# Grouped-query decode attention: larger units, one uniform TensorE loop, and the last weights loaded last

## The chip, the cores and the metric

The kernel runs on one core of a Trainium2 chip. The metric is the device time of one execution in microseconds (us). The span in a profile is the time from the first to the last instruction; the times are 1.7 to 2.9 us longer. One core is in use, so there is no second die to compare with: a run is called slow when it is over 1.5% above the fastest run of its kernel. Ratios are the mean time of one kernel's fast runs over that of the kernel before in the same rounds, so they are not quite the ratios of the medians that I quote.

## The reference

Two attention blocks, A and B, each with batch 4 and one query token. 32 query heads share 8 key heads (4 per key head). The head size is 128, the cache has 8192 keys. A attends to all of them, B only to the last 2048. All data are bf16.

```python
q = (x @ wq).reshape(B, 1, 32, 128).transpose(0, 2, 1, 3)
scores = einsum("bhqd,bhkd->bhqk", q, repeat(k, 4)) * 128 ** -0.5   # B: the last 2048 keys only
o = einsum("bhqk,bhkd->bhqd", softmax(scores), repeat(v, 4))
y = o.transpose(0, 2, 1, 3).reshape(B, 1, 32 * 128) @ wo
# the result: concatenate([A, B], axis=-1)
```

A's K and V are 134 MB, B's 34 MB, the weights 17 MB. Every byte is used once, so the DMA time is a floor.

## The kernel before

Work is cut into 40 units with 2 MB of K and 2 MB of V each: 8 for B (four key heads of one batch), then 32 for A (one key head of one batch). K and V have four slots each. In A a partition holds 64 consecutive keys, one contiguous row of 16 KB.

```python
units = []
for gg in range(HKV // SB):            # B: four key heads
    for b in range(Bn):
        units.append(dict(P=1, b=b, S=2, J=NT // 2, CPT=2 * REP, ...))
for g in range(HKV):                   # A: one key head
    for b in range(Bn):
        units.append(dict(P=0, b=b, S=1, J=NT, CPT=REP, ...))
```

TensorE transposes K (two bf16 keys ride as one fp32), VectorE and ScalarE copy the result out of PSUM, TensorE multiplies it with the queries (S), and the weighted values (PV) follow one unit later. A unit's order on TensorE is this list:

```python
TOKENS = [("T", 0), ("T", 1), ("OT",), ("T", 2), ("T", 3), ("S", 0), ("S", 1), ("X",),
          ("T", 4), ("T", 5), ("S", 2), ("S", 3), ("PV", 0), ("PV", 1), ("OL",),
          ("T", 6), ("T", 7), ("S", 4), ("S", 5), ("PV", 2), ("PV", 3), ("S", 6), ("S", 7), ("OPJ",)]
```

A slot is loaded again when TensorE has read it. The last two K are loaded one after the other, ahead of the last three V:

```python
def sp_K(u):
    waits = [("T", tjob_idx[(u - NKS, NB - 1)])] if u >= NKS else []     # NKS = 4 slots
def sp_V(u):
    waits = [("PV", (u - NVS) * NQ + NQ - 1)] if u >= NVS else []        # NVS = 4 slots
```

TensorE loops over 28 of A's units, four units a turn, to keep its program short. B's query is made first; A's query is made in pieces within B's units.

## Time and profile before

| | before |
|---|---|
| time, median | 449.34 us (448.96 to 450.16, 4 runs) |
| span | 447.8 us |
| DMA data packets | from 1.8 to 440.2 us |
| tail after them | 7.6 us |
| mean granted clock | 0.797 |

From the page of the kernel before: busy time of the engines, the TensorE clock in tenths, DMA and GB/s in 40 slices of the span, and the chain that ended last by engine.

```profile
PE 373.4 (83%) x6783; PEld 339.4 (76%) x6783; DVE 195.9 (44%) x451; ACT 179.2 (40%) x202; POOL 40.1 (9%) x126
...
PEclk9996569989886899866596689867875986788596
DMA  8999999999999999999999999999999999999991
GB/s 337 411 415 438 413 421 415 420 421 423 423 422 421 425 422 425 424 429 427 427 427 430 430 424 426 430 428 427 429 426 427 426 430 429 426 424 430 430 403 65
...
DMA 54%; PE 35%; issue 4%; ACT 3%; DVE 2%; POOL 0%; ACTq 0%; POOLq 0%
```

The DMA row is full in every slice but the first and the last: the kernel is held by DMA. TensorE is close behind it.

The end, by stretches of 10 us: busy us (and instructions) of PE, PEld, DVE, ACT and POOL, then the granted clock, the DMA share and GB/s.

```profile
420.00:430.00 10.00, 9.94 (x136) 7.80 (x135) 4.20 (x9) 4.24 (x5) 0.94 (x3) 0.68 1.01 428
430.00:440.00 10.00, 8.94 (x207) 8.45 (x205) 5.80 (x12) 5.50 (x7) 1.15 (x3) 1.00 0.80 326
```

DMA is full until two microseconds before its end.

### The profile page before, as it was taken

To read this page: it belongs to the slowest core of one execution; us is meant where nothing else is said; L and a number is where in the kernel's file an instruction comes from. 1 tells how busy PE (TensorE), PEld (TensorE's weight loads), DVE (VectorE), ACT (ScalarE), POOL (GpSimd) and SP (SyncE) were. 2 spreads that over 40 slices of the span, in tenths; PEclk is the share of its full clock that TensorE was granted. 3 is DMA by queue.
4 is the path that set the end of the run, shared out by engine and by line. 5 is a ranking of instruction groups with operands and counts; after the bars stand their busy time and mean duration, and the time that the engine had idled before them with its cause. 6 is when DMAs were issued, how large, how long until landed. Compare 5 with 4: busy or idle time off the path is not lost.

```text
span 447.8 us, 14767 instructions
## 1 busy us (share of the span) xinstructions
PE 373.4 (83%) x6783; PEld 339.4 (76%) x6783; DVE 195.9 (44%) x451; ACT 179.2 (40%) x202; POOL 40.1 (9%) x126
## 2 busy tenths in 40 slices
PE   0685199899676999988998998899889998988997
PEld 0685199768561898878898887879878987878896
DVE  0354055656440455434363444344443544344363
ACT  1163045435330464434264434334442543435261
POOL 1100000001100011000010001000110100010010
PEclk9996569989886899866596689867875986788596
DMA  8999999999999999999999999999999999999991
GB/s 337 411 415 438 413 421 415 420 421 423 423 422 421 425 422 425 424 429 427 427 427 430 430 424 426 430 428 427 429 426 427 426 430 429 426 424 430 430 403 65
DMA packets 17270, 185.01 MB, mean 413 GB/s; under 512 B 1860, under 2 KB 2392, under 8 KB 4824
## 3 DMA queue, kind: packets, MB, share of 16 engines
q1 hardware_dynamic: 15096, 178.27, 94.4%
q10 hardware_dynamic: 2080, 6.30, 3.5%
q8 instruction: 22, 0.36, 0.3%
q14 instruction: 8, 0.07, 0.0%
q0 software_dynamic: 64, 0.01, 0.0%
HBM read 184.56 MB, written 0.01 MB: 412 GB/s over the span
## 4 chain that ended last, share of the span: by engine, by line
DMA 54%; PE 35%; issue 4%; ACT 3%; DVE 2%; POOL 0%; ACTq 0%; POOLq 0%
DMA K_sb<-in_A_k_cache_dram 41%; PE ps L332 19%; DMA W<-in_A_wq_dram 7%; DMA W<-in_B_wo_dram 6%; PE ps L397 6%; PE ps L371 5%; PE ps L483 3%; ACT KT_sb L341 3%; PE ps L278 1%; DVE KT_sb L340 1%; DVE Dt L543 0%; DVE M L505 0%; ACT PT L554 0%; PE ps L474 0%; PE ps L438 0%
## 5 line engine op out<-in xcount | busy, mean ns | idle before, releaser
L341 ACT ACTIVATE KT_sb<-ps 128x1024 bf16<-128x1024 bf16 x160 | 163.0, 1023 | 244.9 <-PE ps L332 243.1
L332 PE MATMUL ps<-identf,K_sb 128*128 128x128 f32 x1280 | 217.1, 329 | 32.9 <-DMA K_sb<-in_A_k_cache_dram 17.5
L332 PEld LDWEIGHTS ps<-identf,K_sb 128*128 128x128 f32 x1280 | 179.0, 170 | 46.2 <-DMA K_sb<-in_A_k_cache_dram 18.6
L340 DVE COPY KT_sb<-ps 128x512 int32<-128x512 int32 x160 | 110.4, 690 | 138.9 <-PE ps L332 137.7
L397 PE MATMUL ps<-PT,V_sb 128*128 128x4 bf16 (+1 forms) x2560 | 76.2, 165 | 3.6 <-DMA V_sb<-in_A_v_cache_dram 1.8
L371 PEld LDWEIGHTS ps<-RQc,KT_sb 128*128 128x128 bf16 x2048 | 72.9, 100 | 4.5 <-ACT KT_sb L341 1.2
L371 PE MATMUL ps<-RQc,KT_sb 128*128 128x8 bf16 x2048 | 74.3, 167 | 0.9 <-ACT KT_sb L341 0.8
L397 PEld LDWEIGHTS ps<-PT,V_sb 128*128 128x128 bf16 x2560 | 70.8, 97 | 3.9 <-DMA V_sb<-in_A_v_cache_dram 2.0
L575 POOL PARTITION_ALL_REDUCE LB<-L x40 | 17.3, 432 | 155.2 <-DVE L L566 155.2
L514 POOL PARTITION_ALL_REDUCE MB<-M x32 | 11.9, 371 | 173.3 <-DVE M L505 173.3
L483 PE MATMUL ps<-W,OL 128*4 128x512 bf16 x60 | 22.5, 537 | 4.8 <-DMA W<-in_B_wo_dram 4.8
L592 DVE TENSOR_TENSOR OTg<-ps,RL 128x4 bf16<-128x4 f32 (+1 forms) x40 | 6.9, 173 | 40.2 <-PE ps L397 40.2
L505 DVE TENSOR_REDUCE M<-ps 128x4 f32<-128x256 f32 (+1 forms) x40 | 19.1, 477 | 10.8 <-PE ps L371 10.8
L566 DVE TENSOR_REDUCE L<-PT 128x4 f32<-128x256 bf16 (+1 forms) x40 | 21.9, 547 | 3.3 <-ACT PT L554 2.8
L371 PE MATMUL ps<-RQB,KT_sb 128*128 128x16 bf16 x512 | 18.6, 171 | 2.1 <-issue 1.2
L371 PEld LDWEIGHTS ps<-RQB,KT_sb 128*128 128x128 bf16 x512 | 17.9, 99 | 3.0 <-issue 1.5
L554 ACT ACTIVATE PT<-Dt 128x256 bf16<-128x256 f32 (+1 forms) x40 | 18.1, 452 | 4.0 <-DVE Dt L543 2.0
L483 PEld LDWEIGHTS ps<-W,OL 128*4 128x4 bf16 x60 | 5.6, 104 | 15.3 <-issue 8.7
L278 PE MATMUL ps<-xT,W 128*128 128x4 bf16 x256 | 7.4, 165 | 10.9 <-DMA W<-in_A_wq_dram 10.6
L278 PEld LDWEIGHTS ps<-xT,W 128*128 128x128 bf16 x256 | 7.0, 101 | 11.1 <-DMA W<-in_A_wq_dram 10.7
L543 DVE TENSOR_TENSOR Dt<-ps,MB 128x256 f32<-128x256 f32 x32 | 13.3, 415 | 0.5 <-POOL MB L514 0.5
L257 PE MATMUL ps<-ident,xo_sb 4*128 4x4 bf16 x8 | 0.6, 170 | 14.2 <-POOL identf L617 14.2
(49 smaller groups left out, 64.6 us busy)
## 6 DMA issues: line engine op xcount, KB each, us to landing
K_sb<-in_A_k_cache_dram SPq DMA_DIRECT2D x32, 2048.0 KB, 32.0
V_sb<-in_A_v_cache_dram SPq DMA_DIRECT2D x31, 2048.0 KB, 36.0
K_sb<-in_B_k_cache_dram SPq DMA_DIRECT2D x16, 1024.0 KB, 28.2
V_sb<-in_B_v_cache_dram SPq DMA_DIRECT2D x16, 1024.0 KB, 28.2
W<-in_B_wq_dram SPq DMA_DIRECT2D x1, 4096.0 KB, 12.9
W<-in_A_wq_dram SPq DMA_DIRECT2D x1, 4096.0 KB, 30.0
W<-in_A_wo_dram ACTq DMA_DIRECT2D x8, 512.0 KB, 10.5
W<-in_B_wo_dram SPq DMA_DIRECT2D x1, 2048.0 KB, 29.1
```

Of the source, the lines that this page charges most:

```text
L278: ins = pe.matmul(out=bk[:, hl * Bn:(hl + 1) * Bn], lhsT=W1wq[:, c, hq * DH:(hq + 1) * DH], rhs=xT[:, P, c, :], start=(c == 0), stop=(c == ...
L332: ins = pe.transpose(out=bkf[:, pi * 128:(pi + 1) * 128], in_=K_sbf[:, slot, t0:t0 + 2, :].rearrange("p t d -> p (t d)"), identity=identf[ ...
L340: return e.tensor_copy(out=KT_sb.bitcast(I32)[:, tj % NKT, :], in_=bkf.bitcast(I32)[:, :])
L341: return e.activation(out=KT_sb[:, tj % NKT, :], in_=bk[:, :], func=ACTF.Copy)
L371: ins = pe.matmul(out=stb[:, t * CPT:(t + 2) * CPT], lhsT=ktv[:, pi, :, e], rhs=rhs, start=(e == 0), stop=(e == 1))
L397: ins = pe.matmul(out=otb[:, s * CPT:(s + 1) * CPT], lhsT=V_sb[:, vs, t, :], rhs=pt_cols(u, t * CPT, CPT), start=(j == 0), stop=(j == J - 1))
L483: ins = pe.matmul(out=opb[0:Bn, 0:D], lhsT=OL[:, i // REP, i % REP, :], rhs=wo_view[:, wg + i // REP, i % REP, :], start=(P == 1 and first ...
L505: return dve.tensor_reduce(out=M1[:, 0:NC].rearrange("p (s h) -> p s h", h=CPT), in_=stb[:, 0:NT * CPT].rearrange("p (s j h) -> p s h j", ...
L543: return dve.tensor_tensor(out=Dt[:, 0:NT * CPT].rearrange("p (s j h) -> p s j h", s=S, h=CPT), in0=stb[:, 0:NT * CPT].rearrange("p (s j h ...
L554: return act.activation(out=PT[:, u % NPT, 0:NW], in_=Dt[:, 0:NW], func=ACTF.Exp, scale=scale)
L566: return dve.tensor_reduce(out=L1[:, 0:NC].rearrange("p (s h) -> p s h", h=CPT), in_=PT[:, u % NPT, 0:NT * CPT].rearrange("p (s j h) -> p ...
L575: return pool.partition_all_reduce(LB[:, 0:NC], L1[:, 0:NC], channels=128, reduce_op=ReduceOp.add)
```

## The change

The intent: fewer and longer DMA rows in A (32 KB instead of 16), one form for all units, one TensorE loop over everything, and an end in which the last bytes to land (1 MB of output weights) need little work. There are 20 units with 4 MB of K and 4 MB of V: 4 for B (all eight key heads of a batch) and 16 for A (two key heads of a batch). K and V have two slots each. The core of the diff, with cuts:

```diff
-    NKS, NVS, NKT, NPT = 4, 4, 4, 4
+    units = [dict(P=1, b=b) for b in range(Bn)]
+    units += [dict(P=0, b=b, gp=gp) for gp in range(NSEG) for b in range(Bn)]
...
-        K_sb = sb("K_sb", [128, NKS, NT, DH], BF16)          # 4 slots of 2 MB
-        V_sb = sb("V_sb", [128, NVS, NT, DH], BF16)
+        K_sb = sb("K_sb", [128, 2, NT, DH], BF16)            # 2 slots of 4 MB
+        V_sb = sb("V_sb", [128, 2, NT, DH], BF16)
...
+        for P in (1, 0):                                     # both queries ahead of the loop
+            pe_job_xT(P)
+            for i in range(NQP):
+                pe_job_QP(P, i)
+            pe_job_perm(P)
+        op("pe", None, waits=[("E", perm_idx[0]), ("setup",)])
...
+        TOK = []
+        pc = 0
+        for k in range(NJ):                                  # NJ = 16
+            TOK.append(("T", k))
+            if k < 2:
+                TOK.append(("PV", k))
+                pc += 1
+            else:
+                TOK.append(("S", k - 2))
+                if pc < NC:                                  # NC = 8
+                    TOK.append(("PV", pc))
+                    pc += 1
+        TOK += [("S", NJ - 2), ("S", NJ - 1)]
...
+                else:                                        # values two units behind, of nothing at first
+                    pe_PV(u - 2, tok[1], waits=[("V", u - 2) if u >= 2 else None] if tok[1] == 0 else [])
...
+            w = [("T", tjob_idx[(u - 2, NJ - 1)])] if kind == "K" else [("PV", (u - 2) * NC + NC - 1)]
...
+        for P in (1, 0):                                     # 8 MB of query weights ahead of the first K
+            op("sp", dma(V_sb[:, 1 - P, :, :].rearrange("p t d -> p (t d)"), WQ[P]...), inc=("WQ", P))
+        kv_load("K", 0)
+        for u in range(1, NU + 1):
+            if u < NU:
+                kv_load("K", u)
+            kv_load("V", u - 1)
...
+        for i, n in enumerate(WCH):                          # the last 1 MB of output weights, behind the last V
+            op("sp", dma(Wl_sb[:, h0:h0 + n, :], src), inc=("WL", i))
...
-            with nc.Fori(0, len(turns), engines=[mybir.EngineType.PE]):      # 7 turns of 4 units
+            with nc.Fori(0, n_turn, engines=[mybir.EngineType.PE]):          # 10 turns of 2 units
```

To be uniform the loop also does work on zeros: the values of units -2 and -1, and three turns of output projection.

## The prediction

> **What bounds it now.** DMA. The page's DMA row is full throughout; the table of stretches has the 16 engines at 1.00 to 1.02 through the A phase (426 to 430 GB/s). The trace's packet records: 8064 packets of 16 KB take 614 ns (median), 4096 of 8 KB 311, 256 of 32 KB (query weights) 1218, 4 KB 159, 1 KB 46. Over 16 engines all come to about 437 us; they run from about 2 to 440 us. Then a tail of 7.6 us: the last values (118 matmuls, 3.3 us), normalisation, 8 output matmuls (1.9), copy, store (about 1.7). TensorE is nearly co-limiting: 83% busy at a mean granted clock of 0.797. Its transposes of K follow the clock (8 take 0.93 us at full, 1.8 to 2.0 at half), which alternates between 1.0 and 0.5, as the Trainium skill, "TensorE: Matmul & The Clock Gate", Part 1, has it, and falls after waits for K.
>
> **What the change does.** The bytes stay. One row of 32 KB for two of 16 KB saves 2 x 614 - 1218 = 10 ns: 4032 pairs over 16 engines, 2.5 us. Fewer semaphore packets and instruction fetches save some tenths. B keeps 8 KB rows. DMA work falls from about 437 to 434 us. TensorE's counts stay: 1280 transposes, 2560 score and 2560 value matmuls, with more columns, but 24 to 25 ns each sets the pace. Max, subtract and exp of 1024 columns should take 1.25, 1.25 and 1.1 us (estimates from the two sizes before: 0.42/0.70, 0.42/0.70, 0.42/0.64 us for 256/512); VectorE and ScalarE stay near half busy. Look-ahead stays 8 MB each for K and V, so I expect no DMA hole before the last unit, although TensorE's transposes start at about 31 us instead of 19.
>
> **The critical path is the end.** The last 1 MB of output weights goes behind the last V (3.0 us that hide final work). But the last K lands about 22.7 us before the DMA's end (near 415 us), and its unit is twice as long: transposes, scores and the values of two units back, about 16 us at full clock, 24 at half; then max, reduce, mask, subtract, exp 4.75 us (was 1.8), 128 value matmuls 3.4, normalisation 0.6, 16 output matmuls 1.9 to 3.7 (were 8), copy and store 2.2. That ends 29 us (full clock) to 37 us (half) after the last K: a span of 444 to 452, about 446 for a mixed clock. The last V may also start late: its slot comes free in the middle of that unit, about when the V before it lands: a DMA hole of 0 to 4 us. So the gains of 3 us (DMA) and 2 to 3 us (late weights) are mostly eaten by the longer last unit.
>
> Time is span plus 1.9 us: **448.0 us, range 444.5 to 452.5**. Faster by over 2%: 0.03; within 2%: 0.94; slower by over 2%: 0.03.
>
> **Right if:** DMA at 1.0 until about 415 us, about 431 GB/s in the A phase; 32 KB packets near 1218 ns; TensorE, not DMA, leads the chain of waits over the last 25 us; a dip of DMA near 425 us.
>
> **Wrong if:** the clock stays at half, TensorE falls behind and DMA shows holes mid-run (slower); or the clock is full in the last unit and the span is under 444; or 32 KB packets of K and V are slower than those of the weights.

## More of the kernel before

The three groups that make up TensorE's work, before: transposes (L332), scores (L371) and values (L397); then the line of the waits that shows TensorE waiting for K in A (total us, times, longest us).

```profile
L332 PE MATMUL ps<-identf,K_sb 128*128 128x128 f32 x1280 | 217.1, 329 | 32.9 <-DMA K_sb<-in_A_k_cache_dram 17.5
...
L397 PE MATMUL ps<-PT,V_sb 128*128 128x4 bf16 (+1 forms) x2560 | 76.2, 165 | 3.6 <-DMA V_sb<-in_A_v_cache_dram 1.8
...
L371 PE MATMUL ps<-RQc,KT_sb 128*128 128x8 bf16 x2048 | 74.3, 167 | 0.9 <-ACT KT_sb L341 0.8
```

```profile
PE ps L332 <- DMA K_sb<-in_A_k_cache_dram: 17.5, 13, 2.8
```

TensorE runs out of keys 13 times, 17.5 us in all.

## The result

| | before | after |
|---|---|---|
| time, median | 449.34 us | 470.23 us (467.78 to 478.07, 4 runs) |
| ratio of fast runs | | 1.0442 (1.0406 to 1.0478) |
| span | 447.8 us | 468.8 us |
| DMA idle between its first and last data | 3.6 us | 17.3 us |
| DMA at work in that time | 434.8 us | 438.2 us |
| tail after the last data | 7.6 us | 11.4 us |
| mean granted clock | 0.797 | 0.789 |

The change made the kernel 4.4% slower. The middle rows are worked out from the trace's packet records: at every nanosecond I count the packets in flight, at most 16, and take the missing share as idle. The 21 us of span are 13.7 us of DMA idleness, 3.4 us of DMA work and 3.8 us of tail.

The page of the changed kernel, the same rows as before:

```profile
PE 404.3 (86%) x7074; PEld 370.4 (79%) x7074; DVE 234.0 (50%) x417; ACT 184.8 (39%) x183; POOL 29.8 (6%) x76
...
PEclk9999959599999675958876676789576869857596
DMA  8999999979999999999999999999999999999290
GB/s 359 406 415 421 411 419 419 355 291 407 445 403 420 431 445 417 434 439 403 433 433 408 428 439 428 391 434 407 419 425 417 431 386 433 431 420 394 87 382 2
...
PE 78%; DMA 7%; ACT 6%; issue 5%; DVE 4%; SPq 1%; PEld 0%; PEldq 0%
```

The chain turned over: DMA led 54% of it before and 7% now, TensorE 35% before and 78% now. The GB/s row dips at slices 8 and 9 (355, 291) and nearly stops at slice 38 (87). In between it is restless, 386 to 445, where it was smooth.

The DMA idleness of the changed kernel is 7.4 us up to 420 us, 4.6 of them in the one hole at 80 to 100 us, and 9.4 us after 420 (instruction fetches counted as work).

The same groups, then the longest waits of TensorE:

```profile
L252 PE MATMUL KT<-identf,K_sb 128*128 128x128 f32 x1280 | 268.3, 347 | 26.4 <-issue 12.7
...
L285 PE MATMUL S<-RQc,KT_sb 128*128 128x16 bf16 x2560 | 117.9, 174 | 13.0 <-ACT KT_sb L261 13.0
L299 PE MATMUL OT<-PT,V_sb 128*128 128x8 bf16 x2688 | 93.4, 167 | 1.2 <-issue 1.2
```

```profile
PE S L285 <- ACT KT_sb L261: 13.0, 20, 0.7
...
PE KT L252 <- issue: 12.7, 9, 1.5
...
PE KT L252 <- DMA K_sb<-in_B_k_cache_dram: 5.0, 1, 5.0
```

The last line counts most: TensorE waits for K once, for the very first one. The 13 waits of before are gone, so TensorE is behind from its first transpose (34.5 us, before 19.0) to its last. Two new pauses repeat: 0.65 us at the end of each of the 20 units (the last scores wait for the last copy) and 1.4 us at nine ends of a turn of the loop.

Two pieces of TensorE's timeline in the changed kernel: the end of a turn and the first half of the next unit, then a piece from the second half of the same unit (start, us from start to end, line, out<-in, count).

```profile
281.83 0.36 PE L285 MATMUL S<-RQc,KT_sb 128*128 128x16 bf16 x8 [0.65 <-ACT KT_sb L261]
283.60 0.66 PE L252 MATMUL KT<-identf,K_sb 128*128 128x128 f32 x4 [1.41 <-issue]
284.09 0.55 PE L299 MATMUL OT<-PT,V_sb 128*128 128x8 bf16 x16
...
288.11 0.57 PE L299 MATMUL OT<-PT,V_sb 128*128 128x8 bf16 x16
288.54 1.09 PE L252 MATMUL KT<-identf,K_sb 128*128 128x128 f32 x4
289.42 0.41 PE L285 MATMUL S<-RQc,KT_sb 128*128 128x16 bf16 x8
...
299.89 0.64 PE L252 MATMUL KT<-identf,K_sb 128*128 128x128 f32 x4
300.36 0.35 PE L285 MATMUL S<-RQc,KT_sb 128*128 128x16 bf16 x8
```

Four transposes take 0.64 to 0.66 us at full clock and 1.09 at half. The clock's record has it at half from 285.2 us on, 1.6 us after the pause at the turn's end, for 13.7 us in which TensorE waited for nothing.

By stretches, the two holes of the DMA (columns as before; the last two are the DMA share and GB/s):

```profile
80.00:90.00 10.00, 10.00 (x181) 9.61 (x180) 5.66 (x7) 4.25 (x5) 0.77 (x2) 0.52 0.95 364
90.00:100.00 10.00, 9.35 (x156) 9.00 (x154) 4.45 (x8) 4.89 (x5) 0.00 (x0) 0.80 0.62 223
...
430.00:440.00 10.00, 10.00 (x189) 9.53 (x186) 7.79 (x11) 4.02 (x4) 0.77 (x2) 0.60 0.42 180
440.00:450.00 10.00, 9.40 (x111) 7.55 (x111) 3.95 (x12) 3.07 (x3) 0.00 (x0) 0.72 0.71 273
```

TensorE is busy for 9.4 to 10 of every 10 us in both holes. The DMA waits for TensorE to give slots back.

The end of the changed kernel, from the last scores on:

```profile
452.47 0.36 PE L285 MATMUL S<-RQc,KT_sb 128*128 128x16 bf16 x8 [0.65 <-ACT KT_sb L261]
452.86 1.22 DVE L376 TENSOR_REDUCE M<-S 128x8 f32<-128x1024 f32 x1 [1.46 <-PE S L285]
454.07 3.45 PE L299 MATMUL OT<-PT,V_sb 128*128 128x8 bf16 x128 [1.24 <-issue]
...
456.25 1.06 ACT L415 ACTIVATE PT<-Dt 128x1024 bf16<-128x1024 f32 x1 [3.83 <-PE OT L299]
...
457.45 1.86 PE L615 MATMUL S<-oacc,identf 4*4 4x256 f32 x4
...
459.25 3.57 PE L299 MATMUL KT<-PT,V_sb 128*128 128x8 bf16 x128
...
463.41 3.20 PE L636 MATMUL S<-Wl_sb,OT_sb 128*4 128x256 bf16 x16 [0.59 <-DVE OT_sb L452]
```

The last K has landed at 425.1 us. TensorE begins that unit at 430.0, 4.9 us late, ends its scores at 452.8, and the span ends at 468.8: 43.7 us after the last K. The last exp is done at 457.3, but its values wait until 459.25, because four fp32 matmuls that carry earlier sums into PSUM stand in between.

### The profile page after: what moved, and what is told of

It is laid out like the page before. It is cut to its first block, busy times and chain, and to the rows that moved or that the text cites. A ratio compares the mean times of both kernels' runs of the same rounds, so it can differ in the third digit from the quotient of the medians.

```text
span 468.8 us, 15187 instructions
## 1 busy us (share of the span) xinstructions
PE 404.3 (86%) x7074; PEld 370.4 (79%) x7074; DVE 234.0 (50%) x417; ACT 184.8 (39%) x183; POOL 29.8 (6%) x76
## 4 chain that ended last, share of the span: by engine, by line
PE 78%; DMA 7%; ACT 6%; issue 5%; DVE 4%; SPq 1%; PEld 0%; PEldq 0%
PE KT L252 47%; PE OT L299 13%; PE S L285 11%; DMA K_sb<-in_B_k_cache_dram 7%; ACT KT_sb L261 4%; PE KT L350 4%; DVE L L422 2%; DVE KT_sb L260 1%; ACT PT L415 1%; PE KT L299 1%; PE S L636 1%; DVE ORx L316 1%; SPq L517 1%; PE KT L329 0%; PE S L615 0%
## 5 line engine op out<-in xcount | busy, mean ns | idle before, releaser
L252 PE MATMUL KT<-identf,K_sb 128*128 128x128 f32 x1280 | 268.3, 347 | 26.4 <-issue 12.7
L261 ACT ACTIVATE KT_sb<-KT 128x1024 bf16<-128x1024 bf16 x160 | 163.9, 1024 | 251.6 <-PE KT L252 251.6
L252 PEld LDWEIGHTS KT<-identf,K_sb 128*128 128x128 f32 x1280 | 176.1, 174 | 33.5 <-issue 17.9
L260 DVE COPY KT_sb<-KT 128x512 int32<-128x512 int32 x160 | 110.3, 689 | 145.7 <-PE KT L252 145.7
L285 PEld LDWEIGHTS S<-RQc,KT_sb 128*128 128x128 bf16 x2560 | 122.0, 105 | 25.1 <-ACT KT_sb L261 14.8
L285 PE MATMUL S<-RQc,KT_sb 128*128 128x16 bf16 x2560 | 117.9, 174 | 13.0 <-ACT KT_sb L261 13.0
L299 PE MATMUL OT<-PT,V_sb 128*128 128x8 bf16 x2688 | 93.4, 167 | 1.2 <-issue 1.2
L299 PEld LDWEIGHTS OT<-PT,V_sb 128*128 128x128 bf16 x2688 | 85.5, 101 | 3.4 <-issue 1.3
L422 DVE TENSOR_REDUCE L<-PT 128x8 f32<-128x1024 bf16 (+1 forms) x20 | 40.1, 2005 | 2.5 <-ACT PT L415 2.5
L376 DVE TENSOR_REDUCE M<-S 128x8 f32<-128x1024 f32 (+1 forms) x20 | 24.5, 1225 | 29.2 <-PE S L285 29.2
## 6 DMA issues: line engine op xcount, KB each, us to landing
K_sb<-in_A_k_cache_dram SPq DMA_DIRECT2D x16, 4096.0 KB, 17.3
```

Of the source, the lines that this page charges most:

```text
L252: ins = pe.transpose(out=bkf[:, pi * 128:(pi + 1) * 128], in_=K_sbf[:, slot, t0:t0 + 2, :].rearrange("p t d -> p (t d)"), identity=identf[ ...
L260: return e.tensor_copy(out=KT_sb.bitcast(I32)[:, tj % NKT, :], in_=bkf.bitcast(I32)[:, :])
L261: return e.activation(out=KT_sb[:, tj % NKT, :], in_=bk[:, :], func=ACTF.Copy)
L285: ins = pe.matmul(out=stb[:, t * C:(t + 2) * C], lhsT=ktv[:, pi, :, e], rhs=RQc[:, u % 2, t // TS, e, :], start=(e == 0), stop=(e == 1))
L299: ins = pe.matmul(out=otb[:, s * C:(s + 1) * C], lhsT=V_sb[:, slot, t, :], rhs=PT[:, slot, t * C:(t + 1) * C], start=(j == 0), stop=(j == ...
L376: return dve.tensor_reduce(out=M1[:, 0:n].rearrange("p (s h) -> p s h", h=C), in_=S_ps[u % 2][:, :].rearrange("p (s j h) -> p s h j", s=S, ...
```

## The experiments

Theory A: TensorE sets the pace from its late start to the end and the DMA follows it. Rival D: the two 4 MB slots starve the DMA whatever TensorE does. Later rivals are named where they come up. "Written out" means that TensorE's loop is replaced by straight code.

| run | what differs | median us | ratio to before |
|---|---|---|---|
| after | | 470.2 | 1.044 |
| a1 | loop written out | 464.3 | 1.029 |
| a2 | a1, no work on zeros | 461.2 | 1.023 |
| a3 | a2, first transposes at 25 us instead of 34 | 462.3 | 1.028 |
| a4 | after, half the score matmuls | 456.2 | 1.014 |
| b1 | before, first K 4 MB later | 449.4 | 1.000 |
| c1 | a3, last V in its own buffer | 461.3 | 1.026 |
| c4 | a2, values one unit behind | 469.2, fast runs 462.1 and 463.2 | 1.030 |
| c5 | a2, half of the last unit's transposes | 457.6 | 1.019 |
| d1 | a2, values in a block | 463.1 | 1.029 |
| d2 | a2, values spread over the unit | 497.8 | 1.105 |
| d3 | c1 with d1's block | 465.4 | 1.035 |
| d4 | a2 with useless dense matmuls | 462.7 | 1.028 |
| e1 | a2, last unit's TensorE work cut to a quarter | 453.8 | 1.009 |
| e2 | after, meant to start early, did not | 474.9 | 1.055 |
| e3 | before, last output weights loaded last | 448.3 | 0.998 |
| e4 | after, first transposes at 26 us | 466.5, fast runs 459.5 and 465.6 | 1.030 |
| f1 | c1 with e1's cut | 453.0 | 1.009 |

### Is TensorE the pace? (a1 to a4)

```diff
# a1: emit_pe
-            with nc.Fori(0, n_turn, engines=[mybir.EngineType.PE]):
-                run(turns[0])
+            for o in plan["pe"]:          # all ops, each with its own waits
# a2: a1, and
-                    pe_PV(u - 2, ...)
+                elif u >= 2: pe_PV(u - 2, ...)       # and OT, OL, OPJ only in turns that have a piece
# a3: a2, and
+        WA_sb = sb("WA_sb", [128, DC * HQ * DH], BF16)     # A's query weights, loaded behind K(0), K(1)
+            if u == 2: query(0, ["x", 0, 1])
+            if u == 3: query(0, [2, 3, "p"])
# a4: the changed kernel, pe_S (wrong on purpose)
-                    for e in range(2):  ... start=(e == 0), stop=(e == 1)
+                    for e in range(1):  ... start=True, stop=True
```

> The changed kernel with TensorE's loop written out; same instructions, same order, same waits. Theory A (TensorE sets the pace from its late first transpose at 34.5 us to the end, the DMA only follows): the 9 gaps of 1.4 us at the turns' ends go, 470 falls to about 457 us (455 to 460). Rival D (the DMA sets the pace: slots of 4 MB are given back late and it starves, whatever TensorE's small gaps): within 2 us of 470.

a1: 464.33 us, 6 us less. That is half of what the gaps add up to, and clear of rival D's 2 us. The reason for the half is in its waits: TensorE now waits for K again.

```profile
PE KT L252 <- DMA K_sb<-in_A_k_cache_dram: 20.4, 7, 5.6
```

With 20.4 us of such waits, what TensorE saves in mid-run is no longer passed on. One thing changed besides: all four runs of a1 have a clock of 0.826 to 0.851, against 0.785 to 0.802 in the fast runs of the changed kernel. How much of the 6 us the pauses cost as such, and how much through the clock, is not separated.

> As a1, and the work that only filled the uniform loop is left out: 256 value matmuls in the first two units, and three turns of transposing, spreading and projecting zeros. Theory A: about 10 us of TensorE time less, 445 to 450 us, where the DMA floor of about 436 us plus the end begins to hold. Rival D: no gain over a1 (under 2 us).

a2: 461.17 us, 3 us less again; I had expected 10. Idle DMA up to 420 us is down from 7.4 us to 1.3 (instruction fetches counted as work). What is left lies at the end: about 8 us of DMA idleness between 420 and 449 us, and a tail of 10.2 us.

> As a2, and A's query weights are loaded behind the first two K into their own buffer, A's query made before units 2 and 3, so that TensorE's first transposes come at about 22 us instead of 34.5. Theory A with the late start as its main part: if TensorE is still behind in a2, it gains up to 12 us on a2; if a2 already has TensorE waiting for the DMA, it gains 0 to 4 us: 443 to 448 us. A theory that the late start alone costs the 20 us would have a1 and a2 near 468 and only this one near 450.

a3: 462.25 us, no gain, although the first transposes come 9 us earlier. In a2 TensorE already has slack, and an earlier start is not worth anything then.

> The changed kernel with one of each pair of score matmuls left out (1280 of 2560; the result is wrong on purpose). All DMA, slots, waits and the loop stay. Theory A: 1.6 us of TensorE time less per unit, 470 falls to about 450 us (447 to 455), bounded by DMA and the last unit. Rival D: 466 to 470 us.

a4: 456.18 us, 14 us less, with all slots, waits and the loop unchanged. The holes in mid-run are gone. So it is TensorE's time that starves the DMA, not the slots by themselves: rival D falls as stated. (e4 passes with all scores of A at zero, so the check tells little about scores.)

### Does a late start cost its length? (b1, e2, e4)

```diff
# b1: the kernel before, its DMA order
+        sp_V(0)
+        sp_V(1)
         sp_K(0)
# e4: the changed kernel, A's query not made (wrong on purpose), its weights loaded behind K(1)
-        for P in (1, 0):
-            pe_job_xT(P) ... pe_job_perm(P)
+        pe_job_xT(1) ... pe_job_perm(1)
```

> The kernel before with its first K behind the first two V (4 MB, about 10 us): TensorE's first transposes come at about 29 us instead of 19; the bytes are the same. If a late start as such costs its length: 459 us. If TensorE has slack and catches up (it waits for K 13 times in A): within 2 us of 450.

b1: 449.37 us, ratio 0.9997 (0.9970 to 1.0025). TensorE begins at 29.7 us instead of 19.0, and nothing is lost: it has slack and catches up.

> The changed kernel with its loop and its filler work, but A's query weights loaded behind two K and not used (A's query is made from B's weights, wrong on purpose), so that TensorE's first transposes come at about 25 us instead of 34.5; same bytes. If TensorE, behind all along, passes its late start on to the end: 460 to 463 us. If the late start costs nothing even here: 468 to 471 us.

e2 failed as an experiment. Its first transposes came at 33.3 us, because TensorE's prologue waits for the setup (until 20.7 us) and then makes both queries, which takes until then. It only shows that the late start has a second cause besides the 8 MB of weights. Its 475 us belong to a low clock, 0.770 to 0.782.

> e2 mended: A's query is not made at all (its weights are still loaded, behind two K; A's scores are zero, wrong on purpose), so that TensorE's first transposes really come at about 25 us instead of 34.5; loop and filler work as in the changed kernel. If TensorE passes its late start on to the end: 460 to 463 us. If the late start costs nothing here either: 468 to 471 us, or on the line of time against granted clock that the changed kernel's runs show (466 to 476 us of span for 0.802 to 0.767).

e4: first transposes at 26.2 us. Its two fast runs took 459.48 us (clock 0.817) and 465.63 (0.787); two more took 467.34 (0.776) and 470.34 (0.763). The means of the fast runs are 462.6 us here and 469.4 in the changed kernel, 6.9 us for a start that is 8.3 us earlier. At about the same clock (0.787 against 0.785 and 0.789), one run against two, the difference is 4 to 5 us. So the late start is passed on, about half of it at the same clock, where TensorE has no slack. With b1 and a3 this says: ask who has slack before you count a start. One caution: e4 also spares TensorE about 6 us of query work, which is part of its earlier start.

That the time follows the clock where TensorE is the bound is not shown. The three fast runs of the changed kernel took 467.78, 470.67 and 469.78 us at clocks of 0.802, 0.789 and 0.785 (the slow one 478.07 at 0.767), and the kernel before, held by DMA, spread as far: 447.6 to 450.7 us in its runs beside the experiments, at clocks from 0.778 to 0.807.

### What holds the end? (c1, c4, c5, e1, f1)

Theory E: the end is TensorE's chain behind the last K, a 4 MB unit, then max, exp, values, output. Rival H: the late slot of the last V, and the DMA hole that it makes.

```diff
# c1: a3, and
-  V(L) into V_sb, waits for the values of unit L-2
+  V(L) into WA_sb (free since A's query); the last output weights into V(L)'s slot
# c4: a2, and
-  pe_PV(u - 2, ...) in the first half of a unit
+  pe_PV(u - 1, ...) in the second half
# c5: a2, last unit (wrong on purpose)
-                for pi in range(4):              # four transposes a job
+                for pi in range(2 if u == L else 4):
# e1: a2, last unit: one transpose of four, one pair of scores of four, copies to match (wrong on purpose)
# f1: c1 and e1 together
```

> a3 (written out, no filler work, early start) with the last V loaded into the spare 32 KB buffer, so that it need not wait for the values two units back. Theory E (the end is TensorE's chain behind the last K: a 4 MB unit of some 24 us, then max, exp, values, output): the DMA hole of about 9 us between 420 and 450 us shrinks to about 2, the last V lands some 8 us earlier, and the time stays within 2 us of a3's 462. Rival H (the late slot of the last V and the DMA hole it makes are the cost): 454 us.

c1: 461.3 us, as a3. The hole is gone all the same. The stretches of a3 and then of c1 (DMA share and GB/s last):

```profile
420.00:430.00 10.00, 9.17 (x154) 8.66 (x155) 6.25 (x9) 3.56 (x4) 0.37 (x1) 0.56 0.77 329
430.00:440.00 10.00, 10.00 (x115) 7.83 (x115) 4.46 (x13) 2.51 (x3) 0.40 (x1) 0.59 0.57 215
```

```profile
420.00:430.00 10.00, 9.25 (x149) 8.73 (x150) 4.99 (x7) 3.32 (x4) 0.34 (x1) 0.53 0.95 405
430.00:440.00 10.00, 10.00 (x127) 8.15 (x125) 4.85 (x13) 2.87 (x4) 0.40 (x1) 0.62 0.94 374
```

The DMA share rises from 0.77 and 0.57 to 0.95 and 0.94, the data end at 443.8 us instead of 449.4, and the tail grows from 10.9 to 15.8 us. The hole was in plain sight and cost nothing.

> a2 (written out, no filler work) with the values one unit behind instead of two, in the second half of a unit. It frees V's slots half a unit earlier, takes 128 value matmuls and the 1.9 us seed matmuls off the path after the last exp. Theory E: 457 to 459 us (a2: 461), although the DMA hole at the end is gone. Rival H: about 452 us.

c4 missed: 462.1 to 475.3 us, and 462.1 and 463.2 in its two fast runs, outside both ranges. Its only profile is of a slow run (474.1 us, clock 0.761), so what follows is not shown for the fast ones. There the holes at the end shrank, but TensorE fell behind in mid-run: it waits for K in A only twice (0.6 us), and for copies by VectorE 14.0 us and by ScalarE 7.9 us in its scores. I count it as a worse order on TensorE, not as evidence on the end.

> a2 with 32 of the 64 transposes of the last unit left out (wrong on purpose, may pass by tolerance); no DMA, slot or wait changes. Theory E: the time falls by what 32 transposes take there, 3.7 us at full clock to 7.3 at half: 454 to 457.5 us (a2: 461). Rival H: only the 16 transposes ahead of the last slot's release count: 457.5 to 459.5 us.

c5: 457.55 us, 3.6 us less than a2, at the border of both ranges. It ran in other rounds, on another chip, than a2; by the ratios to the kernel before (1.019 and 1.023) it gains only 1.7 us. It does not tell the theories apart.

> a2 with only a quarter of the last unit's transposes, copies and scores (16 of 64, 32 of 128; wrong on purpose); every load and wait stays. Theory E (what a2 still loses against the kernel before is TensorE's 4 MB unit behind the last K, about 24 us): that unit takes some 9 us, and the time falls from 461 to the DMA's end plus a short tail, 447 to 452 us. Rival: the end is held by loads and slots, or the loss lies mid-run; then it falls by less than 5 us.

e1: 453.82 us, 7.4 us less than a2 and 2 us short of theory E's range. It too ran in other rounds than a2: by the ratios (1.0094 and 1.0226, with their intervals) the gain is about 6 us, between 4 and 8. That is not clear of the rival's 5 us. As far as this shows, TensorE's last unit is more than half of the 10 us that a2 loses to the kernel before, not all.

> c1 (a3 with the last V in its own buffer) with e1's cut of the last unit's TensorE work to a quarter (wrong on purpose). If a2's 11 us over the kernel before are TensorE's last unit (7 us in e1) and the late slot of the last V (what e1 left): 449 to 451 us. If the slot costs nothing even then: 453 to 455 us, as e1.

f1: 452.98 us. Even with TensorE's last unit cut, the slot of the last V is worth 0.8 us at most. The last 3.5 us over the kernel before stay open. The traces say where they lie: in f1 the data end 4.0 us later (444.2 against 440.2 us), the tail is 1.7 us shorter (5.9 against 7.6), and the times are 2.4 to 2.7 us above the span instead of 1.7. Of the 4.0 us, about 2 are instruction fetches of the written-out code (3.8 us in the packet records, over 16 engines, against 1.8) and about 2 more DMA idleness. The 16 output matmuls take 3.57 us where the kernel before has 8 in 1.86, but they lie in the tail that became shorter. No run tests any of this.

### What sets TensorE's clock? (d1 to d4)

The prediction let the clock fall after waits for K. In the changed kernel TensorE never waits for K in A, yet 43% of A's transposes are issued at half clock (37% in the kernel before). The shares by quarter of a unit, counted over A's transposes, are a clue:

| | values are | quarter 1 | 2 | 3 | 4 | all |
|---|---|---|---|---|---|---|
| after | in the first half | 0.35 | 0.69 | 0.69 | 0.00 | 0.43 |
| a2 | in the first half | 0.48 | 0.59 | 0.57 | 0.02 | 0.42 |
| a1 | in the first half | 0.42 | 0.45 | 0.38 | 0.00 | 0.31 |
| c4 (slow run) | in the second half | 0.83 | 0.03 | 0.44 | 0.50 | 0.45 |
| d1 | a block at the start | 0.89 | 0.35 | 0.27 | 0.00 | 0.38 |
| d3 | a block at the start | 0.89 | 0.13 | 0.20 | 0.00 | 0.30 |
| d2 | spread over all | 0.62 | 0.36 | 0.34 | 0.00 | 0.33 |
| d4 | as a2, with dense matmuls between | 0.35 | 0.00 | 0.00 | 0.00 | 0.09 |

Read the last column with care: a1, a2, a3 and c1 have the same order of TensorE's work in A, and their shares run from 0.31 to 0.42 (a3 0.38, c1 0.34). d1, d2 and d3 lie in that spread or at its edge; d4 alone is far outside.

```diff
# d1: TOK = [("PV", 0..7)] then T and S;   d2: ("PV", k // 2) after every second ("T", k), its normalisation moved to k == 14
# d3: c1 with d1's order
# d4: a2, in pe_PV, after each 32nd value matmul
+                    for _ in range(4 if j == TS - 1 and u < L - 1 else 0):
+                        ins = pe.matmul(out=otb[:, 64:512], lhsT=V_sb[:, slot, t, :], rhs=PT[:, slot, 0:448], start=True, stop=True)
```

> a2 with all 128 value matmuls of a unit in one block of 3.3 us at its start, then transposes and scores alone. Theory M (the granted clock follows the mix of the stream about a window later: narrow value matmuls between the transposes bring it to half, whether TensorE waits or not): the share of transposes issued at half clock falls from 0.42 to 0.30 or less, all of it early in the unit, and the time falls by 2 to 8 us from 461. Rival W (as predicted: the clock falls only after waits for K): the share stays near 0.42 and the time at 461.

d1: the share is 0.38, not 0.30, though it lies early in the unit as theory M says; 463.1 us, no gain. The clock is higher in all five runs (0.824 to 0.848, a2 0.792 to 0.817; the profiled run is the lowest), and that bought no time. TensorE now waits more for copies (14.3 and 10.4 us in the scores).

> a2 with the value matmuls spread over the whole unit (16 after every second transpose job). Theory M: the half-clock share of the unit's last quarter, 0.02 in a2, rises to that of the others (0.3 or more); V's slots come free at the unit's end, so the DMA runs dry more and the time is 461 to 470. Rival W: the last quarter stays near 0.

d2: 497.8 us. My sign for the last quarter missed (0.00). The run is of use for something else: with the values at the end of a unit, V's slots come free half a unit later, and the DMA goes idle for 53 us in all. The DMA and GB/s rows of d2:

```profile
DMA  9999999999999986997899699959995999599155
GB/s 361 404 420 422 420 419 422 436 416 411 416 420 425 404 376 255 421 435 331 330 423 421 263 371 449 435 225 414 421 441 203 449 430 422 224 421 448 62 229 196
```

With two slots of 4 MB, half a unit of delay in giving a slot back is the difference between a full DMA and this. So slots do matter; a2's order stays just inside their margin.

> c1 (written out, no filler work, early start, last V in its own buffer) with d1's block: the best of the changed kernel's line so far. If TensorE's chain is all that is left: as much below c1's 461 as d1 is below a2. Hope: 455; the kernel before, 449.5, stays faster.

d3: 465.4 us, no better than c1.

> a2 with 16 useless matmuls of 448 columns per unit among the values (written beside the values' sums and never read): about 3 us more TensorE work per unit at full clock, and a denser stream. Theory M: the half-clock share of transposes falls below 0.2, which gives most of the added work back: 458 to 466 us. Rival W, or a clock that does not care for density: share 0.4 and TensorE behind by up to 3 us per unit: over 480 us.

d4: 462.7 us. The clock row, the transposes and the added matmuls in d4:

```profile
PEclk9999979997998979998998899899989988997995
...
L252 PE MATMUL KT<-identf,K_sb 128*128 128x128 f32 x1280 | 214.9, 294 | 27.1 <-DMA K_sb<-in_A_k_cache_dram 17.5
...
L302 PE MATMUL OT<-PT,V_sb 128*128 128x448 bf16 x288 | 73.1, 380 | 0.0
```

The mean clock is 0.93 instead of 0.79, the share of transposes at half clock falls from 0.42 to 0.09, and the transposes' busy time from 260.1 us (a2) to 214.9. 288 useless matmuls with 73 us of busy time cost the kernel 1.5 us in the median (2.6 by the ratios). Nothing else was changed, and the pauses stayed: between 200 and 420 us TensorE pauses 20 times for 17.2 us, in the changed kernel 23 times for 18.1. So the density of the stream moves the clock. The Trainium skill, "TensorE: Matmul & The Clock Gate", Part 1, says that a monitor of recent activity sets the clock; d4 agrees. It does not follow that one should add such work: it only paid itself back.

Pauses that are not waits for K are a rival that no run takes away, but the traces of d1 and d3 let one read it, since the values stand in a block there. The clock's record moves in steps of 3.41 us. I take the steps between 120 and 440 us that begin at full clock. Without a value matmul in them, all 70 with up to 1.16 us of pauses are followed by full clock, and all 10 with 1.17 us or more by half. With 80 or more value matmuls in them, all 22 are followed by half, and 7 of these have no pause at all. (15 steps with fewer values went both ways.) So both bring the clock down: pauses of any cause, when they come to about 1.2 us in a step, and a dense stream of value matmuls of 8 columns. In the changed kernel the two add up: before each of its 14 falls stand 0.5 to 2.1 us of pauses, none for K, with 16 to 37 value matmuls.

### The late output weights alone (e3)

```diff
# the kernel before
-        wo_at = {7: [1, 2], 8: [NG - 1]}
+        wo_at = {7: [1, 2]}
...
+        add(wo_load("sp", NG - 1))          # behind the last V
```

> The kernel before with one part of the change alone: the last 512 KB of output weights are loaded behind the last V. The last V lands 1.5 us earlier; TensorE's own chain may hold the end by then: 448.0 to 449.5 us, 0 to 1.5 us below the kernel before.

e3: 448.3 us (446.52 to 449.69, 6 runs), ratio 0.9977 (0.9951 to 1.0004). The tail is 6.0 us instead of 7.6 and the result is correct. It is 1.2 us in the median, inside what was expected and not clear of noise. It has the lowest median of all versions here.

## Why the prediction was wrong

The time was 470.2 us against 448.0 predicted and 452.5 at the top of the range. Two steps failed. The first is the overlap, "I expect no DMA hole before the last unit": TensorE's time for a unit, 21.4 us as it turned out, was never set against the DMA's 20.6, and a1 and a2 win back 9 us of that. The second is the size of the end: 43.7 us behind the last K instead of 29 to 37, of which e1 shows about 6 to be the last unit's work.

- "DMA bounds it now" and "TensorE is nearly co-limiting": right. The second half of the sentence deserved more weight.
- "It falls after waits for K" (the clock): this step failed. The trace of after has the clock at half for 43% of A's transposes without a wait for K in A: other pauses and the narrow value matmuls bring it down as well (d1, d3), and d4 moves it by density alone. I had taken an average clock as something that a TensorE that is behind would raise (the prediction does not spell this out). It does not: TensorE was behind all the time and its clock stayed at 0.79. That is no worse than the kernel before had (0.797): the clock did not fall, it failed to rise. I had 16 us for a unit at full clock and 24 at half, and never set a mixture of them against DMA's time. It took 21.4 us: the output projections, one for two units, follow each other in 42.8 us on average (from 145.8 to 445.3 us in seven turns).
- "I expect no DMA hole before the last unit": failed. DMA needs 19.4 us for 8 MB (128 packets of 32 KB over 16 engines for each of K and V at 1213 ns is 9.7 us) and about 1.2 us for half of 1 MB of output weights (an estimate, at 430 GB/s): 20.6 us. TensorE's 21.4 us left no slack, so the late start, which b1 shows to be free in the kernel before, was passed on (e4), and so were the gaps at the turns' ends and the work on zeros, which I had not priced: 9 us from after to a2. The last K landed at 425.1 us, not near 415.
- "One row of 32 KB for two of 16 KB saves 10 ns": right and slightly low at the median, 1213 ns against 2 x 614. But the mean is 1238 ns, because 32 KB packets often take longer: what lies above the median sums to 6.6 us over 16 engines, against 1.0 us for the 16 KB packets of before and 1.0 us for the 32 KB packets of a4. DMA work did not fall by 3 us, it rose by 3.4. That this comes from a starved queue is only argued: of the packets over 1300 ns after the first 60 us, 38% follow a moment with fewer than 8 packets in flight, of the others practically none; in a2 the long ones that remain do not (1%), and in a1 none of 157 does. So a starved queue is at most a part of it. In a4, with the slots and rows of the changed kernel, DMA work is 432.9 us, 1.9 us less than before: there most of the saving came about.
- "The critical path is the end": right in kind, mis-sized. Predicted 29 to 37 us from the last K to the end, measured 43.7: 4.9 us because TensorE was behind, a unit of 22.8 us (predicted 16 to 24), 4.5 us to the exp (4.75), 1.9 us of fp32 matmuls that I had overlooked, then the values and the output as predicted.
- "A DMA hole of 0 to 4 us" at the last V: it was larger (about 9 us between 430 and 457 us), and a3 and c1 show that such a hole did not matter.
- The listed way to be wrong, "TensorE falls behind and DMA shows holes mid-run", is what came true. I gave slower by over 2% a chance of 0.03.

What stays open: 3.5 us between f1 and the kernel before, why the 32 KB packets took longer, and how many value matmuls count as much as a pause for the clock.

## What to carry to other kernels

When a second engine has as little slack as TensorE had here (17.5 us of waits for K in 447.8), what a change costs that engine must be summed as carefully as what it saves the first: loop turns, filler work, exposed waits at the ends of units, a late start. Slack decides whether those are free (b1, a3) or paid, at least in part (e4). Larger units lengthen the work behind the last transfer, and a visible hole in the DMA there need not be the cost; move it away and look whether the time moves.

## What the Trainium skill lacked or had wrong

- "TensorE: Matmul & The Clock Gate", section "Why this matters for your kernels": its rule against drops of the clock is to have no idle gaps of over about 3 us between bursts of matmuls. Here TensorE has no gap above 1.41 us between 200 and 420 us in the changed kernel and still issues nearly half of its transposes at half clock. In d1 and d3 pauses that came to 1.17 us or more in a step of 3.41 us were enough for half clock. Its second failure mode, frequent short pauses between groups of matmuls, fits a part of the falls, but 7 in d1 and d3 follow a step without any pause, full of 8-column value matmuls. That such narrow matmuls keep the clock down the page does not say. (The 16-column scores are not needed for it: a4 leaves half of them out, and its share is 0.43 all the same.)
- "DMA: Bandwidth & Descriptors", section "Bandwidth": one sentence says that the HBM side, at about 358 GB/s for a core, binds transfers from HBM to SBUF. Taken alone it misleads for a core that streams alone: in A the kernel before moved 419 to 430 GB/s from HBM in every stretch of 20 us from 80 to 400 us (the prediction's 426 to 430 hold only from 180 us on), and packets of 32 KB at 1213 ns on 16 engines are 432 GB/s. The same section says that the 358 are each core's share when both cores of the HBM domain stream, and its table has 425 GB/s for 16 MB on a single core: that agrees.
- No page has times by packet size in a full queue. Here the medians were 46 to 47 ns for 1 KB, 159 to 160 for 4 KB, 309 to 312 for 8 KB, 614 for 16 KB and 1213 to 1218 for 32 KB.
- No page has the cost of a whole turn of a loop on TensorE. Here a turn's end, with its semaphores set back and its branch, cost 1.4 us without a matmul.
